# A fused DeltaNet and SwiGLU kernel: a planner's search with stored moves is replaced by one stored order of all operations

## The chip, the core and the metric

The kernel runs on one core of one Trainium2 chip. The metric is device time in microseconds, the median of several executions; before the change it is 663.25 us (three executions, 663.02 to 663.70). Lower is better. The engines are TensorE (PE; PEld is its weight load), VectorE (DVE), ScalarE (ACT), GpSimd (POOL) and SyncE (SP), which here only issues DMAs.

## What is computed

Two layers follow each other. The first is a DeltaNet recurrence over 4 batches x 8 heads, 768 steps, head size 48:

```
for t in range(S):
    y[:, :, t] = einsum('bhd,bhde->bhe', q[:, :, t], state)
    v_old = einsum('bhde,bhd->bhe', state, kt)          # kt: k[t], normalised
    state = state + bt * einsum('bhd,bhe->bhde', kt, vt - v_old)
```

Its output, turned to 3072 tokens x 384, goes through RMSNorm and a SwiGLU layer (384 to 1536 and back): `(silu(xn @ w_gate) * (xn @ w_val)) @ w_out`, in float32.

## The kernel before, in words

**Staging.** The sequence is cut into 12 chunks of 64 steps. For each chunk the recurrence is done in block form: scores of k with k and of q with k (PE, L705), the inverse of a unit triangular matrix (a chain of short DVE operations; for chunks 0 and 1 L904 and L914, later L1076 and L1085), products with the state and with that inverse, and the update of the state (PE, L1414). The chunk's output is normalised (ACT squares L1439, POOL roots L1464 and L1465), turned (PE L1495, evacuated by DVE L1499) and fed to the feed-forward layer: up products L1568 and down products L1550 for chunks 0 and 1, up products L1661 and down products L1718 (both by a scheme with fewer multiplications) for the other ten. The weights arrive from HBM as 64-bit words and are converted piece by piece by ACT (L620) and three DVE operations (L608, L611, L616 and a sum, L640).

**What sets the order.** The kernel does not issue instructions as it describes the work. It records 3005 operations by `P.add(engine, duration, function, priority, reads, writes, PSUM groups ...)`, and `Plan.run` then calls their functions in an order of its own. Operations are numbered as they are added, 0 to 3004, and the text below uses those numbers. Each engine executes its instructions in the order in which they were issued; semaphores between engines follow from the data. Before the change `Plan.run` searches: `forward` is a list scheduler with the model's durations, which gives PSUM banks to groups as they come free; `backward` and `reorder` make new priorities from its result; `shake` disturbs them from a stored number (`MOVES`, a long list of such numbers). The best of these orders by the model's end is issued.

**Fillers.** Up to 70 us by the model, `run` puts matmuls of the identity (L1836) into gaps of PE that the model expects: before each PE operation it compares the operation's modelled start with the end of the PE operation before (`pe = s + op.dur`), and fills the difference. They write a spare PSUM bank and read `ident`, which POOL makes at the start (`make_identity`, masks.py). The fillers are not operations of the plan.

**Row modes.** Matmuls use all 128 rows, or 64 or 32 (`P.rows`). The model charges a change of mode. Below, a stretch is a run of neighbouring PE operations in 64 or 32 rows between two in 128.

**The operations that the prediction speaks of.**

| number | engine, line in the profile | what it is |
|---|---|---|
| 4, 12, 13 | POOL masks.py, L540 and L543, L549 | `ident`; two masks |
| 18, 19 | ACT queue L488 | loads of the two halves of q of chunk 0 |
| 57, 59, 61 | PE L686, L686, L705 | turn k of chunk 0; its scores |
| 73, 75 to 97 | PE L849; DVE | gather, then the inversion of chunk 0 |
| 34 | DVE L608 | a shift in a weight's conversion |
| 120 to 137 | PE L1305, L1317; DVE L1365 (126 is one of these) | corrections of chunk 0, each waiting for the one before |
| 140, 157 | PE L1327, L1414 | output of chunk 0; state of chunk 0 |
| 141, 142, 149, 150 | ACT L1439 | squares of the output, two for each half |
| 145, 153; 146, 154 | POOL L1464, L1465; DVE L1470 | roots of the two halves; a diagonal made of each |
| 147, 155; 148, 156 | PE L1495; DVE L1499 | turned output of the two halves, and its evacuation |
| 452 | PE L1568 | first product of the feed-forward layer |
| 446, 449 | DVE L716, PE L705 | q of chunk 2 turned; its scores |

Of the kernel before, what the change touches and what calls it, by code (L numbers as in the profile page):

```python
# [25 lines left out]
ROUNDS, MOVES = (11, 17), (11000120, 11000520, 11000860, 11001126, 11001220, 11001422, 11001980, 11002920, 11003160, 11004760, 11005600, 11005880, 11005960, 11006540, 11006780, 11043348, 11046060, 11046762, 11046960, 11047400, 11051200, 11051587, 11052413, 11052800, 11052820, 11052943, 11053820, 11054160, 11059400, 11059520, 11065474, 11067742, 11067873, 11082899, 11089211, 11091393, 11091930, 11092484, 11092500, 11094487, 11095726, 11096934, 11097464, 11100744, 11101720, 11101800, 11103240, 11108560, 11111180, 11112100, 11113200, 11114320, 11115185, 11116472, 11119560, 11123118, 11123844, 11129946, 11130300, 11131636, 11133484, 11135300, 11135580, 11136720, 11137707, 11138500, 11141245, 11141565, 11141800, 11142243, 11143240, 11144659, 11145351, 11145392, 11145780, 11147877, 11159279, 11165300, 11166260, 11168180, 11184780, 11194240, 11199374, 11229385, 11245940, 11251680, 11259120, 11260740, 11758040, 11759220, 11773661, 11773860, 11778240, 11779680, 11781040, 11781305, 11781546, 11782138, 11783153, 11783560, 11792184, 11792893, 11794321, 11796160, 11800685, 11801080, 11823340, 11823372, 11824520, 11825640, 11826356, 11826483, 11826769, 11828197, 11829285, 11829840, 11829894, 11831880, 11837531, 11837960, 11840160, 11842020, 11858050, 11865880, 11866881, 11869703, 11870540, 11871293, 11871355, 11871362, 11871985, 11872236, 11872952, 11873062, 11873083, 11873496, 11874635, 11875943, 11876490, 11877075, 11877540, 11877667, 11879480, 11879491, 11879904, 11879920, 11880840, 11881540, 11881735, 11883480, 11884299, 11884640, 11885160, 11885407, 11885576, 11885889, 11886080, 11886591, 11886963, 11887410, 11887417, 11887780, 11890320, 11891127, 11891657, 11891671, 11891936, 11892084, 11892108, 11892132, 11892631, 11893543, 11895220, 11896940, 11899177, 11899762, 11900189, 11900750, 11937706, 11937985, 11938040, 11938200, 11939661, 11939723, 11939981, 11940060, 11940560, 11940660, 11941080, 11941260, 11941571, 11941681, 11941805, 11941840, 11942094, 11942342, 11942397, 11942428, 11942545, 11942989, 11944696, 11946950, 11953520, 11957695, 11957953, 11958514, 11958552, 11958996, 11959144, 11959433, 11959674, 11960951, 11961240, 11961505, 11961801, 11961911, 12010011, 12010360, 12010414, 12010548, 12011298, 12012255, 12012420, 12012480, 12014554, 12014688, 12015074, 12015201, 12015411, 12015948, 12017200, 12018092, 12018178, 12018202, 12026500, 12027260, 12028280, 12028861, 12031263, 12032385, 12233004, 12233496, 12235764, 12236425, 12237578, 12238320, 12239154, 12239254, 12240228, 12241157, 12241412, 12241522, 12241935, 12308180, 12308572, 12309120, 12309284, 12309540, 12310460, 12310578, 12310695, 12311566, 12311820, 12311831, 12311879, 12312571, 12313342, 12315200, 12315658, 12315665, 12316480, 12317785, 12319360, 12320084, 12320332, 12320440, 12321900, 12322710, 12322882, 12325601, 12325687, 12328265, 12328554, 12329420, 12331555, 12333379, 12336108, 12337380, 12338140, 12338789, 12339901, 12341329, 12341477, 12341501, 12349040, 12350398, 12351375, 12352232, 12354040, 12361697, 12365640, 12376020, 12377201, 12377349, 12379139, 12379314, 12379875, 12380261, 12380340, 12380581, 12380860, 12381180, 12382200, 12382322, 12383802, 12384153, 12384542, 12389320, 12393700, 12397307, 12397830, 12399723, 12400040, 12400370, 12400400, 12400480, 12401240, 12401867, 12402280, 12404120, 12446660, 12449007, 12449038, 12449960, 12449981, 12450820, 12451454, 12452820, 12453130, 12453822, 12453839, 12455133, 12455360, 12455701, 12455983, 12456427, 12457525, 12460237, 12460360, 12462320, 12463760, 12469433, 12472286, 12475683, 12476700, 12477872, 12478481, 12481785, 12485027, 12486160, 12487302, 12490040, 12496240, 12517588, 12518070, 12518335, 12519612, 12520680, 12520840, 12520860, 12520868, 12521866, 12521983, 12522427, 12522575, 12522699, 12522840, 12522878, 12523573, 12523728, 12523852, 12524060, 12524282, 12524296, 12524920, 12525022, 12525080, 12526160, 12526760, 12528973, 12530236, 12531080, 12532067, 12534380, 12546480, 12546818, 12548938, 12548955, 12551939, 12556444, 12557400, 12558140, 12562040, 12585099, 12858147, 12862253, 12862270, 12862525, 12862938, 12863096, 12863564, 12863943, 12865316, 12867209, 12868059, 12868854, 12869081, 12869790, 12870320, 12871308, 12871332, 12871463, 12871614, 12872010, 12872127, 12872430, 12873108, 12874698, 12877706, 12877768, 12878360, 12878377, 12878625, 12878828, 12878838, 12878976, 12879080, 12879788, 12879809, 12879984, 12880652, 12881674, 12882280, 12883646, 12885195, 12885732, 12886062, 12886730, 12888320, 12888480, 12888967, 12890457, 12890705, 12890746, 12890853, 12891018, 12891159, 12891717, 12892016, 12892749, 12894133, 12894518, 12896253, 12896435, 12897671, 12898490, 12898662, 12898669, 12899200, 12899636, 12899901, 12900166, 12900916, 12900947, 12901102, 12902434, 12902458, 12902885, 12903188, 12903439, 12903745, 12904048, 12904120, 12906901, 12906994, 12907049, 12908615, 12914686, 12915509, 12916073, 12921776, 12927995, 12955200, 12956175, 12956223, 12956760, 12957204, 12957899, 12957930, 12958123, 12958746, 12959441, 12959720, 12959761, 12960126, 12960694, 12961131, 12961678, 12962660, 12962800, 12962807, 12962900, 12962986, 12963251, 12963399, 12963554, 12964077, 12964841, 12967360, 12967646, 12970220, 12970520, 12972495, 12973166, 12975434, 12975613, 12979820, 12981144, 12981815, 12982080, 12984090, 12985088, 12986489, 12986661, 12987215, 12988344, 12989218, 12989648, 12993358, 12994012, 12994711, 12994852, 12995461, 12995974, 12996755, 12997134, 12997151, 12998280, 12998297, 13002372, 13002413, 13002802, 13003518, 13003893, 13005077, 13005373, 13005769, 13006200, 13006440, 13007211, 13007930, 13009080, 13010880, 13010907, 13011038, 13011616, 13011640, 13012284, 13012879, 13012996, 13013500, 13013557, 13015388, 13015980, 13017570, 13018262, 13019377)  # L26
BLOCK, ASKED, LACKED = 256, 140, 193
REACT, TURN, LAND = 2.4, 3.45, 2.6
STICK = 1.0
# [5 lines left out]
SHAKE = 0.12  # L35
# [37 lines left out]
class Plan:  # L73
# [39 lines left out]
    def first_priorities(self):  # L113
        for op in reversed(self.ops):
            if op.late:
                op.prio = min(
                    (u.prio - (0.0 if u.eng == op.eng and not op.dma else op.lat + u.slack + 0.2) for u in op.users),
                    default=op.prio,
                ) - STRETCH[op.eng] * op.dur - (3.0 if op.dma else 0.0)
            op.key = op.prio - op.ahead - (2000.0 if op.first else 0.0)  # L120

    def forward(self, banks, until):

        at = dict.fromkeys(ENGINES, 0.0)
        held = {"DVE": 0.0, "POOL": 0.0}
        cand = {e: [] for e in ENGINES}
        free = list(banks)
        for op in self.ops:
            op.wait, op.at = len(op.deps), op.ready
            for g in op.acquire:  # L130
                g.taken, g.uses = False, g.left
                g.reader, g.until = "", 0.0
            if not op.wait:
                cand[op.eng].append(op)
        order, server, end_, mode, slip = [], 0.0, 0.0, 0, 0.0
        self.lag = 0.0
        chain = {e: [] for e in ENGINES}
        for op in self.ops:
            op.was, op.done = op.start, False
            if op.first and op.was is not None:  # L140
                chain[op.eng].append(op)
# [1730 lines left out]
```

## Time and profile before

| | |
|---|---|
| median of three executions | 663.25 us |
| profiled execution, first to last instruction | 659.72 us |
| around it (663.25 less 659.72) | 3.53 us |
| PE busy | 649.0 us, 98% |
| weight loads busy | 603.6 us, 91% |
| DVE busy | 568.3 us, 86% |
| ACT, POOL busy | 295.5 us, 75.0 us |
| DMA issues on SP | 601 |

The profiled execution's own time is not listed apart from its span; its span and the median of the others differ by the 3.53 us that lie around a span. Busy times are sums over the span; a matmul's end is modelled, so the distance from the start of one PE operation to the start of the next says more about PE than its busy share, and the prediction uses such distances, read from the trace. "idle before" names the time that an engine stood still and what ended it.

### The profile page before, as it was taken

The numbers are of one execution on the slowest core, as the hardware profiler recorded it, in microseconds if no ns is written. First come the engines' busy times: TensorE is split into PE (matmuls) and PEld (weight loads), VectorE is DVE, ScalarE is ACT, GpSimd is POOL, SyncE is SP. The second block draws the span as 40 slices with busy tenths as digits, with TensorE's granted clock in tenths as the row PEclk, the third lists the DMA queues.
The fourth block names the chain that finished last, engine by engine and source line by source line (L and its number), as shares of the span: only waits on it lengthen the run. The fifth ranks groups of instructions, "written<-read, shape, count | busy, mean of one in ns | idle before, by whom it ended". The sixth has DMA issues, their size and how long they took to land.

```text
span 659.7 us, 23463 instructions
## 1 busy us (share of the span) xinstructions
PE 649.0 (98%) x10048; PEld 603.6 (91%) x10048; DVE 568.3 (86%) x1211; ACT 295.5 (45%) x681; POOL 75.0 (11%) x95
## 2 busy tenths in 40 slices
PE   8989999999999999999999999999999999999997
PEld 6878877777899999999999999999999999999997
DVE  5999999899899898998998998998999599367372
ACT  7555443224445545345355355345355353353241
POOL 4212201112011030110030120030021001000000
PEclk9999999999999999999999999999999999999999
DMA  9586593524526457466366385376345524301100
GB/s 229 132 214 162 124 246 115 95 35 94 93 42 109 68 135 110 65 153 110 52 152 107 57 164 93 68 154 98 59 110 80 97 46 74 58 26 25 25 1 25
DMA packets 270431, 64.40 MB, mean 98 GB/s; under 512 B 256980, under 2 KB 262135, under 8 KB 270327
## 3 DMA queue, kind: packets, MB, share of 16 engines
q1 hardware_dynamic: 267046, 62.12, 47.2%
q8 instruction: 79, 1.29, 0.8%
q10 hardware_dynamic: 3280, 0.79, 0.6%
q14 instruction: 26, 0.20, 0.1%
HBM read 45.30 MB, written 17.56 MB: 95 GB/s over the span
## 4 chain that ended last, share of the span: by engine, by line
PE 86%; DVE 9%; SPq 2%; issue 1%; ACT 1%; DMA 0%; POOL 0%; POOLq 0%; ACTq 0%; DVEq 0%
PE bank L1661 41%; PE bank L1718 21%; PE bank L1568 6%; PE bank L1550 4%; PE bank L1209 3%; PE bank L705 3%; SPq L488 2%; PE bank L1327 2%; PE bank L1291 2%; PE bank L1414 1%; PE bank L1836 1%; PE bank L1134 1%; PE bank L1162 1%; DVE tmp L616 1%; DVE w_in L640 1%
## 5 line engine op out<-in xcount | busy, mean ns | idle before, releaser
L1661 PE MATMUL bank<-xf,w_in 128*128 128x128 f32 x1440 | 177.4, 276 | 0.0
L1661 PEld LDWEIGHTS bank<-xf,w_in 128*128 128x128 f32 x1440 | 168.8, 192 | 0.9
L1671 DVE TENSOR_TENSOR tmp<-tmp,bank 128x512 f32<-128x512 f32 x180 | 121.3, 682 | 36.9 <-PE bank L1661 32.9
L1661 PE MATMUL bank<-xf,more 128*128 128x128 f32 x960 | 123.4, 277 | 0.0
L1661 PEld LDWEIGHTS bank<-xf,more 128*128 128x128 f32 x960 | 114.9, 192 | 1.3 <-issue 0.2
L1673 ACT COPY tmp<-bank 128x512 f32<-128x512 f32 x120 | 69.1, 585 | 72.2 <-PE bank L1661 52.4
L1677 ACT ACTIVATE tmp<-tmp 128x256 f32<-128x256 f32 x120 | 49.8, 417 | 92.1 <-DVE tmp L1671 91.8
L1085 DVE TENSOR_REDUCE acc<-acc 128x30 f32<-128x90 f32 (+4 forms) x150 | 69.8, 466 | 1.6
L732 POOL TENSOR_TENSOR knrm<-ksum,half 128x16 f32<-128x16 f32 x12 | 35.8, 2983 | 297.0 <-DVE ksum L731 297.0
L1718 PE MATMUL bank<-wo_sb,hf 128*128 128x192 f32 x360 | 63.7, 328 | 0.2 <-DVE hf L1678 0.2
L1718 PEld LDWEIGHTS bank<-wo_sb,hf 128*128 128x128 f32 x360 | 58.1, 190 | 0.8 <-DVE hf L1678 0.4
L1678 DVE TENSOR_TENSOR hf<-tmp 128x256 f32<-128x256 f32 x120 | 50.1, 428 | 9.1 <-ACT tmp L1677 8.4
L1076 DVE TENSOR_TENSOR acc<-acc,at 128x60 f32<-128x60 f32 (+4 forms) x150 | 51.3, 342 | 1.4
L1568 PE MATMUL bank<-xf,w_in 128*128 128x256 f32 x144 | 34.1, 384 | 0.3 <-DVE xf L1499 0.3
L1550 PE MATMUL bank<-wo_sb,hf 128*128 128x384 f32 x96 | 33.3, 488 | 0.0
L1568 PE MATMUL bank<-xp,w_in 128*128 128x256 f32 x144 | 32.9, 381 | 0.2 <-DVE r L1256 0.2
L1106 POOL COPY acc<-acc 128x128 f32<-128x128 f32 x40 | 21.0, 555 | 100.1 <-DVE acc L1085 86.9
L1568 PEld LDWEIGHTS bank<-xf,w_in 128*128 128x128 f32 x144 | 26.7, 190 | 5.3 <-issue 0.6
L1568 PEld LDWEIGHTS bank<-xp,w_in 128*128 128x128 f32 x144 | 27.0, 190 | 4.7 <-DVE r L1256 0.3
L1550 PEld LDWEIGHTS bank<-wo_sb,hf 128*128 128x128 f32 x96 | 17.9, 190 | 9.9
L1575 ACT ACTIVATE tmp<-bank 128x256 f32<-128x256 f32 x24 | 9.2, 383 | 38.8 <-PE bank L1568 36.7
L1520 DVE TENSOR_TENSOR xf<-xf 128x256 f32<-128x256 f32 (+1 forms) x70 | 24.0, 382 | 2.8 <-ACT xf L1505 1.2
(198 smaller groups left out, 967.0 us busy)
## 6 DMA issues: line engine op xcount, KB each, us to landing
at<-dkk SPq DMA_DIRECT2D x20, 256.0 KB, 3.7
more<-in_moe_w_gate_dram SPq DMA_DIRECT2D x6, 768.0 KB, 7.9
vt<-in_v_dram SPq DMA_DIRECT2D x24, 192.0 KB, 4.4
k<-in_k_dram SPq DMA_DIRECT2D x23, 192.0 KB, 3.9
out_dram<-tmp SPq DMA_DIRECT2D x46, 96.0 KB, 2.2
more<-in_moe_w_val_dram SPq DMA_DIRECT2D x5, 768.0 KB, 4.3
more<-in_moe_w_out_dram SPq DMA_DIRECT2D x5, 768.0 KB, 5.3
dsq<-k SPq DMA_DIRECT2D x6, 512.0 KB, 2.8
```

Of the source, the lines that this page charges most:

```text
L732: P.add("POOL", 2.95, lambda: nc.gpsimd.tensor_tensor(out=knrm[i2], in0=ksum[i2], in1=half, op=ALU.pow), pn, r=[("ksum", i2), "half"], w=[ ...
L1076: nc.vector.tensor_tensor(out=acc[:, 1:3, 0:n, j + 2 : W].rearrange("p a i t -> p i a t"), in0=acc[:, old, 0:n, j : j + 2, None].to_broadc ...
L1085: nc.vector.tensor_reduce(out=acc[:, new, 0:n, j + 2 : W], in_=acc[:, lo : lo + 3, 0:n, j + 2 : W].rearrange("p a i t -> p i t a"), axis=A ...
L1520: P.add("DVE", V(128 * n), lambda dst=dst, a=a, b_=b_, op=op: nc.vector.tensor_tensor(out=dst, in0=a, in1=b_, op=op), pxv, r=[("xp", 0)], ...
L1550: nc.tensor.matmul(po[p].t[:, 0:DM], hf[:, spot(f), 128 * p : 128 * p + 128], wo_sb[:, spot(f)], start=(f == f0), stop=(f == f1 - 1), skip ...
L1568: nc.tensor.matmul(ps.t[:, TOK * side : TOK * side + TOK], w_in[:, side, h_, 3 * t + i_, n : n + 128], x_[:, 2 * t : 2 * t + 2].rearrange( ...
L1661: nc.tensor.matmul(g.t[:, 128 * z : 128 * z + 128], fac[:, side, 128 * f : 128 * f + 128], xf[:, xs], start=(begin and z == 0), stop=False ...
L1671: P.add("DVE", V(512), lambda t=t, g=g: nc.vector.tensor_tensor(out=t, in0=t, in1=g.t, op=ALU.add), -1, r=[g], w=[tk], last=g)
L1673: P.add("ACT", A(512), lambda t=t, g=g: nc.scalar.copy(t, g.t), -1, r=[g], w=[tk], last=g)
L1677: P.add("ACT", A(256), lambda t=t: nc.scalar.activation(out=t[:, 0:256], in_=t[:, 0:256], func=ACTF.Silu), -1, w=[tk])
L1678: P.add("DVE", V(256), lambda t=t, f0=f0, p=p: nc.vector.tensor_tensor(out=hf[:, spot(f0) : spot(f0) + 2, 128 * p : 128 * p + 128], in0=t[ ...
L1718: nc.tensor.matmul(g.t[:, 0:192], a_[:, f], b_[:, f], start=(begin and f == 0), stop=(f == 5), skip_group_check=True)
```

## The change

No operation is added or taken away, and no duration, buffer or DMA is changed. `MOVES` and the search (`first_priorities`, `forward`, `backward`, `reorder`, `shake`) go. A string `ORDER` lists all 3005 operations, and `run` goes through it once, keeping the model's clock only to hand out PSUM banks and to place the fillers. Three details of `run` differ too: the time from which a filler is counted is now the modelled end with everything in it (`pe = end`, which includes a wait for PE's own instructions and a change of mode) and not `s + op.dur`; the bank that came free first is taken by the same model; and the bank release is timed by that end.

```diff
-ROUNDS, MOVES = (11, 17), (11000120, 11000520, 11000860,
...
+ORDER = """
+17 1 13 16 5 12 7 0 4 77 2 3 10 11 6 19 8 15 18 31 9 22 213 14 50 51 57 52 59 32 58 53 60 54 55 61 106 63 62 108 38 64 107 73 69 21 56 70 67 20 203 74
...
+"""
...
-    def run(self, free, filler=None, until=0.0):
-        self.first_priorities()
...
-        for op, s in best[1]:
-            op.start = s
...
-            if filler and op.eng == "PE":
-                if s < until:
-                    filler(fillers(pe, s))
-                pe = s + op.dur
-            op.fn()
...
+        for op in (self.ops[int(n)] for n in ORDER.split()):
+            e = op.eng
+            s = max(op.at, at[e])
...
+            end = s + op.dur
+            if e == "PE":
...
+                if s < until:
+                    n = fillers(pe, s)
+                    filler(n)
+                    count += 4 * len(n)
+                if op.size:
+                    late, asked = supply(s, op.dur, count, op.size)
+                    count += op.size + (0.5 if op.size in (16, 128) else 0.0)
+                    end += late
+                pe = end
...
+            op.fn()
```

What moves, by a comparison of the two programs as built: on PE 286 of 570 operations stand at another place, by 9 places at most; on DVE 970 of 1176, by up to 53; on ACT 345 of 615, by up to 8; on POOL 6 of 43, by up to 2; on SP 544 of 601, by up to 39. The largest DVE shifts lie between 60 and 190 us. The fillers are 14 matmuls instead of 16, with 3840 columns instead of 4608. Lines of the new kernel are 58 lower (the filler is L1778).

In the front of the program these moves matter to the text below:

```
            before                                  after
POOL        4, 12, 13                               13, 12, 4
ACT         77 213 (18 19: DMAs) 10 52              77 10 (19 18: DMAs) 213 52
DVE         84 34 85 ... 97                         84 85 ... 97
DVE         97 to 126, 34, 215 and 216 not in it    97 to 126, with 34, 215 and 216 in it
ACT         141 142 161 149 150                     141 142 149 150 161
DVE         148 164 156                             148 156 ... 164
PE          157, filler (768 columns), 147 155      157 147 155
PE          481 482 627 449 340 344 630             481 344 340 482 449 630 627
SP          last two q loads behind second at       all q loads of chunk 2 ahead of second at
```

More of the change, by code (lines that the diff above doesn't have):

```diff
@@ L2 @@
 import math
-import random
 from contextlib import ExitStack
@@ L111, in add, with run, supply @@
         return op
[L113 to L122, printed above, removed]
+    def run(self, banks, filler=None, until=0.0):
         at = dict.fromkeys(ENGINES, 0.0)
         held = {"DVE": 0.0, "POOL": 0.0}
-        cand = {e: [] for e in ENGINES}
-        free = list(banks)
+        free = sorted(banks, key=lambda x: x[0])
         for op in self.ops:
-            op.wait, op.at = len(op.deps), op.ready
+            op.at = op.ready
             for g in op.acquire:
[L131 to L141, printed above, removed]
-        for e in ENGINES:
-            chain[e].sort(key=lambda op: -op.was)
-        count, asked, usable = 0.0, -9.0, {}
-        def supply(s, dur, n0, size, keep):
+                g.uses = g.left
+        server, mode, count, asked, usable, lanes, pe = 0.0, 0, 0.0, -9.0, {}, [0.0] * 8, 0.0
+        def supply(s, dur, n0, size):
             late, last, got = 0.0, asked, {}
@@ L161, in supply @@
                         late += max(0.0, got.get(k, usable.get(k, 0.0)) - t)
[L162 to L163 removed]
+            usable.update(got)
             return late, last
[L165 to L200 removed]
@@ L201, in forward @@
+        for op in (self.ops[int(n)] for n in ORDER.split()):
+            e = op.eng
+            s = max(op.at, at[e])
+            if op.dma:
+                s = max(s, lanes[0])
+            for g in op.banks:
+                if g.reader != e:
+                    s = max(s, g.until)
+            if op.port:
+                s = max(s, held["POOL" if e == "DVE" else "DVE"])
             for g in op.acquire:
-                if not g.taken:
-                    g.taken = True
-                    free.pop(0)
@@ L205, in forward @@
-            op.start = s
+                if g.t is None:
+                    t, g.t = free.pop(0)
+                    s = max(s, t)
             if op.mode is not None and op.mode != mode:
                 s += DRAIN if op.mode < 128 else REFILL
-                op.start, mode = s, op.mode
+                mode = op.mode
             end = s + op.dur
-            if op.eng == "PE":
+            if e == "PE":
                 if s - at["PE"] > 1.4 and s > until:
@@ L345 @@
+                u.at = max(u.at, (end + TIED if e == "DVE" and not u.loose else at[e]) if u.eng == e and not op.dma else end + op.hop(u) + u.slack)
+        self.end = max(at.values())
 @with_exitstack
```

145 lines of the change are left out of this document (6 added, 139 removed), and 92 rows, old and new, of the table ORDER.

## The prediction

> **What bounds the kernel now.** First the stretches of the span, with each engine's busy time (columns: PE, PEld, DVE, ACT, POOL, granted clock, DMA share, GB/s).
>
> ```profile
> 6.90:20.00 13.10, 11.83 (x277) 9.25 (x275) 9.50 (x33) 10.44 (x19) 2.92 (x1) 1.00 0.91 226
> 20.00:41.00 21.00, 18.44 (x527) 16.35 (x528) 19.98 (x51) 10.55 (x26) 6.13 (x7) 1.00 0.73 189
> 41.00:100.00 59.00, 57.80 (x1085) 48.48 (x1085) 56.62 (x109) 29.06 (x59) 7.39 (x4) 1.00 0.71 181
> ...
> 150.00:655.00 505.00, 504.77 (x7779) 487.26 (x7778) 430.79 (x908) 224.53 (x536) 47.90 (x63) 1.00 0.45 83
> ```
>
> From 150 to 655 us PE is never idle (504.77 of 505 us): whatever order its instructions have, it does the same matmuls, and only a price that depends on its neighbours can change. Before 41 us PE waits for a chain, and from 20 us DVE is full (19.98 of 21). So an order can gain in the first 41 us, by changes of row mode, and by the few waits left. From the first up product (452, at 40.74 us) the starts add up to 613.0 us; the shortest distances seen for the same operation with the same neighbours add up to 606.0.
>
> Next the timeline of the start and of 33 to 41 us (start, duration, engine and line; in brackets the idle time before).
>
> ```profile
> 0.79 0.20 POOL masks.py:197 MEMSET ident<- 128x128 f32 x1 [0.29 <-POOLq L1856]
> ...
> 1.07 0.29 POOL masks.py:199 TENSOR_SCALAR_AFFINE_SELECT ident<-ident 128x128 f32<-128x128 f32 x1
> ...
> 1.31 0.10 POOL L540 MEMSET below<- 128x3 f32 x1
> ...
> 1.42 4.21 PE L1836 MATMUL bank<-ident 128*128 128x512 f32 x6 [1.42 <-POOL below L540]
> 1.49 0.42 POOL L543 TENSOR_SCALAR_AFFINE_SELECT below<-below 64x3 f32<-64x3 f32 x2
> ...
> 1.96 0.31 POOL L549 MEMSET wsum<- 128x256 f32 x1
> ```
>
> PE starts as soon as `ident` is done, and its first six filler records hold it until 5.42, when 57 starts; k had landed at 5.08.
>
> ```profile
> 33.83 0.26 PE L1414 MATMUL bank<-u,k 64*48 64x48 f32 x4
> 35.58 0.92 PE L1414 MATMUL bank<-u,k 64*48 64x48 f32 x60 [1.49 <-issue]
> 36.43 1.57 PE L1836 MATMUL bank<-ident 128*128 128x512 f32 x6
> 37.84 0.39 PE L1495 MATMUL bank<-xp,yn 128*128 128x128 f32 x2
> ```
>
> Operation 157 stops after four matmul records for its own instructions, takes 2.60 us to the next start where a later one takes 0.83, and then a filler keeps 147 back for 1.41 us, although its inputs were there at 35.66.
>
> ```profile
> 35.39 0.33 ACT L1439 ACTIVATE xp<-bank 128x192 f32<-128x192 f32 x1 [0.51 <-DVE acc L914]
> ...
> 39.18 0.95 DVE L616 SCALAR_TENSOR_TENSOR more<-hf,more 128x768 f32<-128x768 uint32 x1
> ...
> 40.05 0.55 DVE L1499 TENSOR_TENSOR xf<-bank,g_sb 128x384 f32<-128x384 f32 x1
> ...
> 40.74 1.97 PE L1568 MATMUL bank<-xf,w_in 128*128 128x256 f32 x8 [0.27 <-DVE xf L1499]
> ```
>
> The last evacuation (156) stands behind a weight conversion: its matmuls ended at 39.39, it starts at 40.05.
>
> **The change part by part.** Durations are those of the profiled execution.
>
> *1. `ident` made third (+0.85).* On POOL L549 (0.31), L540 (0.10) and L543 (0.42) now stand ahead; with the gaps between (0.1 us in all) `ident` is ready 0.93 later, so the first filler starts at 2.35. It is the same filler (4.0 us), so 57 starts near 6.3 instead of 5.42. 57, 59, 61, the spread of the scores (L775, L777), the gather and the inversion hang on it one behind another. Cover: q of chunk 0 lands at 9.33, and 108 holds back the gather now; that hides 0.2 at the gather, but ACT's four operations behind 61 shift fully. Between 0.4 and 0.93; I take 0.85, near full, as the chain has no other slack.
>
> *2. DVE between 14 and 31 us (+0.5).* Taking shift 34 (0.55) out of the inversion frees 0.38 (85 started at 15.48 and could at 15.10). But 97 (end 19.98) to 126 (29.82) is DVE without a pause, and there 34, 215 and 216 come in: 0.55 + 0.39 + 0.25, less 0.09 of overlap each, = 0.92. So 126, and with it 127 to 157, comes 0.92 - 0.38 = 0.5 later. Between 0.4 and 0.6.
>
> *3. No filler after 157 (-1.4) and the second half's evacuation (-0.5).* With 1 and 2, 157 starts at 33.83 + 1.35 = 35.2, and with the same stop ends at 37.8; 147 follows at once: 37.8 against 37.84. The second half: ACT does 149 and 150 straight behind 140 (35.4 to 36.2, no waiting for DVE), POOL's root 153 follows 145 (36.65 + 1.57 = 38.2), 154 takes 0.28, 155 starts at 38.6 (38.51 before) and ends 0.88 later. 156 follows at 39.5, not behind the 0.95 of L616, and 452 starts at 40.2 instead of 40.74. The first three parts together: **-0.5**. The stop in 157 has the same instructions ahead of it (11 filler matmuls before and after the change), so I keep 1.77; without it the chain over 154 binds and at most 0.4 more would come.
>
> *4. Fewer changes of row mode (-1.2).* A group of L1661 starts 0.893 after its like, but needs 0.987 ahead of a 64-row operation and 0.995 behind one; scores (L705) take 1.091 ahead of 128 rows and 0.982 ahead of another 64-row operation. So a stretch joined to another saves 0.094 + 0.102 + 0.11 = 0.31. From 452 on there are 62 stretches before and 58 after: 4 x 0.31 = 1.2. If the 32-row ones save only the first two, 0.8.
>
> *5. The scores of chunk 2 (-0.4).*
>
> ```profile
> 80.17 0.58 SPq L488
> ...
> 80.80 0.45 SPq L488
> ...
> 81.29 3.15 DMA vt<-in_v_dram
> 84.44 0.02 issue
> 84.45 1.24 DVE qt L716
> ```
>
> Their turned q (L716) waits for the last two q loads, which SP issues behind the second load of `at` (78.80, 1.32 us); 627 ahead of 449 takes 2.24 instead of 0.97, a wait of 1.27. With all q loads ahead of that load the wait is gone; but 344 and 340 move ahead of 482, and 344 needs ACT's result of 83.30, when PE, 0.5 early, is there at 81.6 with the old times. ACT shifts early with the rest by 0.5, so some 0.9 to 1.2 comes back. Between -1.27 and +0.4; I take -0.4.
>
> *6. The rest (0).* DVE and SP are mixed most between 60 and 190 us. PE's waits there, besides that of part 5, are 0.25, 0.23 and 0.1 us, though DVE stands idle for only 2.4 us between 41 and 100. The two loads of k that hold SP from 84.7 to 93.7 are issued some 35 us later, which clears the queue. The cover gone would cost up to those 2.4 us. The tail (3.9 us behind the last PE operation) only swaps two stores between queues: 0.
>
> Sum: -0.5 (parts 1 to 3, at 452) - 1.2 - 0.4 = **-2.1 us**. The span of 659.72 becomes 657.6; with 3.53 us around it, and against the median of 663.25, **661.2 us**. A difference of 0.2% (1.33 us) is about what this measurement can tell from none.
>
> **The clock.** The first filler's 512-column records start 0.85 apart, later ones 0.43, and the L686 records change from 0.213 to about 0.11 at 6.7 us: PE runs at half speed for 5.3 us after its first matmul (1.42). [...]
>
> **Rivals.** *A, q later (to 663.6).* ACT now issues the q loads behind a second table load and an activation; if the queue holds them until those are done (copy to 3.47, table 1.28, activation 0.20), they go at 5.0 and 5.6 instead of 1.64 and 2.30. Landing is then between 10.2 (the first load's 4.64 us) and 12.6 (the second's 7.03); the gather follows 1.1 behind, at 13.7 instead of 11.3 at worst: 0 to +2.4. Against: at 1.64 the queue has already passed a table load and two copies. [...] Chance 0.1.
>
> *B, full clock later (662.7).* If the later first matmul delays full speed past the gather, 61 and 106 to 73 run at half speed: about +1.1 for 61 and +0.4 for what of the others isn't hidden, so -0.6. Against: nothing in one trace shows the rise moving by more than the start does. [...] Chance 0.07.
>
> *C, nothing to gain (662.6).* PE is full from 41 us and parts 3 and 5 turn into other waits: only part 4 is left, less 0.5: -0.7. For it: 41 to 100 us, DVE 96% busy. Chance 0.12.
>
> *D, slower (664.7).* PE stops for its own instructions where dense 64-row operations follow one another, as in 157: 1.77 us each time. The new order has four runs of three (before: one of three, one of four); two such stops make -2.1 + 3.5 = +1.4, and from two on it is slower. Against: other runs of 64 rows (two L705 at 350 us, 2.02 us together) pass without a stop. Chance 0.12.
>
> *E, the late start costs little (659.9).* If q's landing or the clock's rise hides half of it, part 1 falls to 0.4 (-0.45); with part 5 in full (-0.87 more) that is 659.9. Chance 0.14.
>
> **How the numbers follow.** Forecast 661.2, chance 0.45 with 660.3 to 661.9. Faster by over 0.2% (under 661.92): 0.45 + E 0.14 = 0.59. Within 0.2%: A, B, C = 0.29. Slower (over 664.58): D 0.12. Range 659.4 (E, and no stop in 157) to 664.0, which leaves out most of D and little else.
>
> **What will show it.** First filler (L1778) at 2.35 and L628 at 6.3; no L1778 between L1356 and L1437 near 37.8; first L1510 near 40.2; ACT's L1381 four in a row; the last PE operation about 2.1 us earlier. Wrong if the gather (L791) comes after 12 us (A), if L1603 groups show idle "issue" above 1 us (D), or if PE stands waiting for DVE by more than 1 us in all between 41 and 165 us (C).

## The result, and the profile after

| | before | after |
|---|---|---|
| median, 22 executions each | 663.26 us | 666.09 us |
| lowest, highest | 661.75, 667.19 | 662.98, 669.44 |
| profiled execution, span | 659.72 us | 663.3 us |
| start of operation 452 | 40.74 us | 39.73 us |
| start of the last PE operation | 653.74 us | 657.33 us |

The ratio is 1.0035 (95% interval 1.0021 to 1.0050): slower by 0.35%, where 661.2 us was forecast and the range ended at 664.0. In the profiled executions the new order gains 1.0 us up to operation 452 and loses 4.6 us behind it.

In the new kernel scores are L647 (they were L705), the turns (transpositions) of loaded q and k on DVE L658 (L716), the up products L1603 (L1661), the DVE sums that feed them L1613 (L1671). First the stretches, with the columns of the prediction's first fence.

```profile
20.00:41.00 21.00, 18.35 (x530) 16.68 (x530) 19.66 (x50) 10.94 (x28) 6.34 (x7) 1.00 0.64 181
41.00:100.00 59.00, 57.13 (x1141) 47.57 (x1140) 54.86 (x106) 29.77 (x60) 7.59 (x4) 1.00 0.62 156
150.00:655.00 505.00, 500.79 (x7745) 483.12 (x7736) 429.11 (x904) 223.05 (x534) 47.29 (x63) 1.00 0.46 82
```

In the stretch where PE was never idle before (504.77 of 505 us) it now stands 4.21 us. The start, and 33 to 41 us, in the timeline:

```profile
1.69 0.20 POOL masks.py:197 MEMSET ident<- 128x128 f32 x1
1.96 0.29 POOL masks.py:199 TENSOR_SCALAR_AFFINE_SELECT ident<-ident 128x128 f32<-128x128 f32 x1
...
2.31 3.69 PE L1778 MATMUL bank<-ident 128*128 128x512 f32 x6 [2.31 <-POOL ident masks.py:199]
...
34.40 0.26 PE L1356 MATMUL bank<-u,k 64*48 64x48 f32 x4
...
35.05 0.92 PE L1356 MATMUL bank<-u,k 64*48 64x48 f32 x60 [0.39 <-issue]
...
36.28 0.94 PE L1437 MATMUL bank<-xp,yn 128*128 128x128 f32 x6 [0.31 <-DVE xp L1412]
...
39.73 1.53 PE L1510 MATMUL bank<-xf,w_in 128*128 128x256 f32 x6
```

`ident` comes late, as the diff said; no filler stands between 157 (L1356) and 147 (L1437) any more, and 452 (L1510) starts a microsecond earlier. What PE waited for behind 41 us, by the view of waits (engine, line, releaser: us in total, times, longest):

```profile
PE bank L1104 <- DMA mt<-dx: 1.3, 1, 1.3
PE bank L647 <- DVE qt L658: 1.2, 1, 1.2
PE bank L647 <- DVE kt L658: 1.0, 1, 1.0
PE bank L1603 <- DVE tmp L1613: 0.9, 1, 0.9
PE bank L1104 <- ACT tmp L1665: 0.5, 1, 0.5
PE bank L1076 <- DMA m1bd<-dxt: 0.4, 1, 0.4
...
```

The same view of before has four lines:

```profile
PE bank L705 <- DVE qt L716: 1.1, 1, 1.1
PE bank L1568 <- DVE xf L1499: 0.3, 1, 0.3
PE bank L1718 <- DVE hf L1678: 0.2, 1, 0.2
PE bank L1568 <- DVE r L1256: 0.2, 1, 0.2
```

In the changed kernel the second is operation 449 at 85.6 us, which had its wait in the trace of before as well. The other five of those shown lie between 261 and 467 us, where the kernel before has none above 0.2. The table gives each operation's step, the distance from the start of the PE operation ahead of it to its own start:

| operation | starts at | step: shortest of all traces with this PE order, and here | what ended the wait |
|---|---|---|---|
| 1253, L1076 | 261.6 us | 2.05, 2.54 us | loads of `m1bd` |
| 1314, L1603 | 298.0 us | 0.89, 1.97 us | DVE, which stood at a turn |
| 1912, L647 (scores) | 351.7 us | 0.99, 2.07 us | DVE's turn 1911, behind loads from `dsq` |
| 1866, L1104 | 366.6 us | 2.04, 2.57 us | ACT |
| 2366, L1104 | 467.2 us | 2.15, 3.56 us | a DMA |

Together the five steps are 4.6 us above the shortest. (The other steps behind 452 gain and lose some 0.8 us each, so that the loss there is 4.6 us too.)

Operation 1314 in the timeline:

```profile
288.01 2.46 SPq L430 DMA_DIRECT2D q<-dsq  x3
...
290.58 1.57 SPq L430 DMA_DIRECT2D dyn<-yn  x2
...
292.19 0.56 SPq L430 DMA_DIRECT2D q<-dsq  x1
...
293.71 0.68 DVE L1613 TENSOR_TENSOR tmp<-tmp,bank 128x512 f32<-128x512 f32 x1
...
296.09 1.25 DVE L658 STREAM_TRANSPOSE kt<-q 128x1024 f32<-128x1024 f32 x1 [1.70 <-DMA q<-dsq]
297.25 3.04 DVE L1613 TENSOR_TENSOR tmp<-tmp,bank 128x512 f32<-128x512 f32 x5
...
297.96 1.16 PE L1603 MATMUL bank<-xf,more 128*128 128x128 f32 x8 [0.91 <-DVE tmp L1613]
```

SP issues the last of four q loads behind two stores of yn. DVE stands 1.70 us at the turn (operation 1661) until that load has landed, and the L1613 group behind it starts only then, at 297.25 us. PE needs neither load nor turn there: it needs the L1613 that stands behind the turn. The kernel before has the same DVE operations around the turn, and no wait:

```profile
294.99 1.24 DVE L716 STREAM_TRANSPOSE kt<-q 128x1024 f32<-128x1024 f32 x1
296.15 2.61 DVE L1671 TENSOR_TENSOR tmp<-tmp,bank 128x512 f32<-128x512 f32 x4
```

New are the times: the last q load was issued at 290.97 us before, at 292.19 in the changed kernel, and DVE came to the turn at 294.99 us before, at 294.39 in the changed kernel.

### The profile page after: what moved, and what is told of

Read it like the earlier page. It is cut to its first block, busy times and chain, and to the rows that moved or that the text cites. A ratio compares the mean times of both kernels' runs of the same rounds, so it can differ in the third digit from the quotient of the medians.

```text
span 663.3 us, 23462 instructions
## 1 busy us (share of the span) xinstructions
PE 646.5 (97%) x10044; PEld 601.3 (91%) x10044; DVE 569.9 (86%) x1211; ACT 294.8 (44%) x681; POOL 74.8 (11%) x95
## 4 chain that ended last, share of the span: by engine, by line
PE 84%; SPq 5%; DMA 4%; DVE 3%; issue 2%; ACT 1%; POOL 1%; ACTq 0%; DVEq 0%
PE bank L1603 36%; PE bank L1660 20%; PE bank L1510 8%; SPq L430 5%; PE bank L1492 4%; PE bank L647 3%; PE bank L1151 3%; PE bank L1269 2%; PE bank L1233 2%; DMA q<-dsq 1%; PE bank L1356 1%; DMA vt<-in_v_dram 1%; PE bank L1104 1%; PE bank L1259 1%; PE bank L1076 1%
## 5 line engine op out<-in xcount | busy, mean ns | idle before, releaser
L1603 PE MATMUL bank<-xf,w_in 128*128 128x128 f32 x1440 | 178.6, 276 | 0.0
L1603 PEld LDWEIGHTS bank<-xf,w_in 128*128 128x128 f32 x1440 | 169.4, 192 | 0.9 <-issue 0.2
L1613 DVE TENSOR_TENSOR tmp<-tmp,bank 128x512 f32<-128x512 f32 x180 | 121.7, 681 | 37.8 <-PE bank L1603 30.8
L1603 PE MATMUL bank<-xf,more 128*128 128x128 f32 x960 | 124.8, 277 | 0.9 <-DVE tmp L1613 0.9
L1603 PEld LDWEIGHTS bank<-xf,more 128*128 128x128 f32 x960 | 115.2, 192 | 2.6 <-DVE tmp L1613 1.1
L1510 PE MATMUL bank<-xf,w_in 128*128 128x256 f32 x144 | 33.8, 384 | 0.1
L1510 PE MATMUL bank<-xp,w_in 128*128 128x256 f32 x144 | 33.0, 382 | 0.3 <-DVE hf L1518 0.3
L1510 PEld LDWEIGHTS bank<-xf,w_in 128*128 128x128 f32 x144 | 26.6, 190 | 5.6 <-issue 0.5
L1510 PEld LDWEIGHTS bank<-xp,w_in 128*128 128x128 f32 x144 | 26.9, 190 | 5.0 <-DVE hf L1518 0.7
```

The source lines that it names most:

```text
L1510: nc.tensor.matmul(ps.t[:, TOK * side : TOK * side + TOK], w_in[:, side, h_, 3 * t + i_, n : n + 128], x_[:, 2 * t : 2 * t + 2].rearrange( ...
L1603: nc.tensor.matmul(g.t[:, 128 * z : 128 * z + 128], fac[:, side, 128 * f : 128 * f + 128], xf[:, xs], start=(begin and z == 0), stop=False ...
L1613: P.add("DVE", V(512), lambda t=t, g=g: nc.vector.tensor_tensor(out=t, in0=t, in1=g.t, op=ALU.add), -1, r=[g], w=[tk], last=g)
```

## Experiments

All kernels use the changed `run`, so an experiment is another `ORDER` (noq and pool also change the issue of some DMAs). "Old" and "new" are the two orders; a part of one is followed by what is left of the other, in its own sequence. Ratios are against the kernel before, on the same chip.

**Theory:** the five waits between 245 and 480 us are the loss, and they come from the order there. **Rivals:** the start (late `ident`, fewer fillers, the clock); the details of `run`; the order of PE alone or of SP alone.

### Where the loss lies

```diff
 border     ORDER = old
 fa_rb      ORDER = new up to 452         + rest of old
 fb_ra      ORDER = old up to 452         + rest of new
 a250_b     ORDER = new up to 245 us      + rest of old
 bab        ORDER = old up to 452, new up to 245 us, rest of old
 bba        ORDER = old up to 248 us      + rest of new
```

> The order of the kernel before, written out as ORDER in the changed kernel's run. Theory (the waits of the new order between 41 and 655 us): nothing of the loss is left, the median within 1 us of before's 663.3, last PE start near 653.7 us. Rival (the details of run: counting of fillers with pe = end, banks handed out by the same clock): 665 us or more, and the fillers of the start differ.

> The new order up to operation 452 (the first up product), then what is left in the order of before. Theory: only the gain at 452 stays (39.73 against 40.75 us, so -1.0), less about 0.3 where the two orders are joined: 662.3 to 663 us. Rival (the later ident, the missing filler and the clock at the start cost the time): 665 to 666 us, and executions at a granted clock of .995 as often as in the changed kernel (7 of 22).

> The order of before up to operation 452, then what is left in the new order. Theory: the whole loss of the middle without the gain of the front: 2.8 + 1.0 over before, 667 us, with waits for DMA at the same operations (1314, 1912, 2366). Rival (the start): 663.3 us. If the waits hang on the 1 us by which 452 comes earlier, PE here would be late enough for the DMAs and most of the waits would shrink: 664 to 665 us.

> The new order up to the 245th us of its model, then what is left in the order of before. Theory: the loss arises behind 250 us (waits of 0.4, 1.1, 1.2, 0.5 and 1.5 us between 259 and 464 us), so those go and the balance at 250 us (about 0, with the front's -1.0 and +1.0 behind it) stays: 662.5 to 663.7 us. Rival (the start, or the waits at 54 and 77 us, carry it): 665 us or more.

> Old order up to operation 452, new order up to 245 us, old order behind. If the gain of the kernel with the new order up to 245 us (660.4) is made in the first 41 us alone, this one is like before, 662.7 us or a little slower (the trace of the old front with the new order behind it lost 1.0 us between 41 and 250 us: 663.7). If the new order between 41 and 245 us gains by itself: 661.5 us or below.

> Old order up to 248 us, new order behind. Theory (the new order behind 245 us loses by itself): before plus 2 to 3 us, 665 to 666 us. Rival (it loses only where the new order stands ahead of it, by 1 to 2 us of earlier work): 663 us.

> The new order up to 245 us and the old behind it, timed a second time. First time 660.4 us, ratio to before 0.9966 (0.9948 to 0.9985). If that was no chance: 660 to 661 us, and in the trace again no wait over 0.5 us behind 100 us.

| to 41 us | 41 to 245 us | behind | run | median | ratio (95%) |
|---|---|---|---|---|---|
| old | old | old | border | 662.62 us | 0.9986 (0.9970 to 1.0003) |
| new | old | old | fa_rb | 663.13 us | 1.0001 (0.9983 to 1.0019) |
| old | new | old | bab | 662.90 us | 0.9996 (0.9979 to 1.0014) |
| new | new | old | a250_b | 660.36 us | 0.9966 (0.9948 to 0.9985) |
| new | new | old | a250_b2 | 661.08 us | 0.9978 (0.9951 to 1.0005) |
| old | new | new | fb_ra | 664.43 us | 1.0018 (0.9995 to 1.0042) |
| old | old | new | bba | 665.51 us | 1.0032 (1.0010 to 1.0053) |
| new | new | new | after2 | 664.49 us | 1.0021 (1.0000 to 1.0042) |

The details of `run` show no cost (border). The new order behind 245 us costs 0.3% behind the old order (bba), 0.2% behind the front of bab (fb_ra against bab, whose intervals overlap) and 0.4 to 0.7% behind the new order (the changed kernel and after2 against a250_b2 and a250_b). The waits differ with what stands ahead: the step to 1314 is 1.3 us and that to 1912 0.9 us above the shortest in bba, which has no wait at 1253, and fb_ra waits 1.6 us at 1253 and 0.2 to 0.3 us at 1314, 1912 and 1866. The new order ahead of 245 us gains 0.3% in one timing and 0.2%, with an interval that reaches 1.0005, in the other; its first 41 us alone (fa_rb) and its middle alone (bab) show no gain. I had expected fa_rb to keep the 1.0 us, and fb_ra to take 667 us. In the trace of fa_rb 452 starts at 41.51 us (a clock dip, below); behind it PE has about 1 us of fillers at 47 to 49 us that the kernel before does not have there, 0.8 us of "issue" at 81 us (border has 1.4 at the same operation) and a wait of 0.7 us for DVE at 92 us. The waits of a250_b behind 41 us, all that the view lists:

```profile
PE bank L1356 <- issue: 0.4, 1, 0.4
PE bank L1510 <- DVE hf L1518: 0.4, 1, 0.4
PE bank L647 <- DVE qt L658: 0.2, 1, 0.2
PE bank L1660 <- DVE hf L1620: 0.2, 1, 0.2
```

None of the five is left, nor in a250_b2, where 449 waits 2.0 us at 86 us. So the start is not the cause; the loss is behind 245 us.

### The start: `ident` first again

```diff
-17 1 13 16 5 12 7 0 4 77 ...      (a250_b)
+17 1 4 13 16 5 12 7 0 77 ...      (a250_id)
```

> The kernel of the new order up to 245 us and the old behind it (660.4 us), with ident first on POOL again. The first filler starts at 1.4 instead of 2.3. By the price of the prediction's part 1: 0.85 less, 659.5 us. If the clock's rise and the landing of q hide most of it (57 started at 5.81 against 5.42): 0.4 less or nothing.

Measured: 661.91 us, ratio 0.9978 (0.9954 to 1.0002), no better than a250_b. 57 starts at 5.42 us, but 452 at 39.66, between the 39.39 and 39.91 of the traces of a250_b and a250_b2. No cost of the late `ident` is seen at 452 or in the time. That is one trace, though, and ten traces with the late `ident` and no clock dip spread from 39.39 to 40.51.

### One DVE instruction, two places later

```diff
-... 1289 1456 1285 1661 1307 1297 1313 ...    (DVE)
+... 1289 1456 1285 1307 1297 1661 1313 ...
```

> The changed kernel with one DVE instruction (1661, the square turn behind the q loads) moved behind the next two DVE operations, 1307 and 1297; SP's order unchanged. Theory (PE at 1314 waited because DVE stood in its order before 1661 for a DMA): PE's wait at 1314 falls from 1.07 to under 0.2 us, though the DMA lands no sooner; about 1 us earlier at operation 1320. Rival (the wait is PE's need of the turned k itself): it stays or moves to operation 1662.

> The changed kernel with the one DVE instruction (1661) two places later, now timed: in its one execution the waits at 1314, 1866 and 2366 were gone, and the span 660.9 against 663.3. If one place on DVE carries the later waits too: 663 to 664 us. If that was the chance of one execution (its 452 started 0.8 us later): -1.1 against the changed kernel, 665 us.

> The changed kernel once more, for its trace and its time beside the others. The waits at 1253, 1314 and 1912 (0.40, 1.07, 1.17 us) hang on the order and come again; those at 1866 and 2366 (0.51, 1.50 us), gone in two executions of a kernel with one DVE instruction moved, hang on long DMA issues that fall elsewhere each time, and are gone here. Time: 665 to 666.5 us. If they come again, the one DVE instruction at 296 us carries them.

Measured: turn296, one execution, 662.58 us; turn296b 663.75 us, ratio 1.0000 (0.9978 to 1.0023), against 1.0035 (from 1.0021) and 1.0021 (from 1.0000) for the changed kernel: the intervals overlap, so the gain rests on the traces. From the timeline of turn296b:

```profile
293.49 0.56 SPq L430 DMA_DIRECT2D q<-dsq  x1
...
293.98 2.29 DVE L1613 TENSOR_TENSOR tmp<-tmp,bank 128x512 f32<-128x512 f32 x3
...
296.27 1.95 PE L1603 MATMUL bank<-xf,more 128*128 128x128 f32 x16
...
296.87 1.25 DVE L658 STREAM_TRANSPOSE kt<-q 128x1024 f32<-128x1024 f32 x1 [0.60 <-DMA q<-dsq]
```

The load is issued 1.3 us later than in the changed kernel, and PE no longer waits: DVE does the L1613 first that PE needs. So PE waited because DVE stood at the turn, as the theory had it. The DVE order is not what is new there, as the kernel before has the turn at the same place: what is new is a later load and an earlier DVE, and an earlier load cures the wait as well (fix4 and spB, below). In both traces of this kernel the step to 1314 is 0.89 us, and the 0.5 us at 1866 are gone too. Whether those hung on the same stall is open: the steps to 1314 and 1866 are 2.19 and 2.08 us in bba, 1.18 and 2.49 us in noq. In after2, the changed kernel again, the steps to 1314 (2.38 us), 1912 (2.07), 1866 (2.44) and 1253 (2.44) come again; the 1.4 us at 2366 do not (2.15 us, as in ten of the 13 traces with that PE order; two show 2.24 and 2.41). The longest wait of the profiled execution was chance.

### The order of SP

```diff
 spB     PE, ACT, DVE, POOL: new; SP behind 245 us: old
-new     ... 1416 1221 1415 1143 1417 1418 1225 1226 ...
+fix4    ... 1225 1226 1416 1221 1415 1143 1417 1418 ...
-new     ... 1387 1386 1659 ...
+fix4    ... 1659 1387 1386 ...
-new     ... 1735 1910 1639 1908 1909 1907 ...
+fix4    ... 1910 1908 1909 1907 1735 1639 ...
-new     ... 2141 2224 2419 2223 2213 2221 2222 ...
+fix4    ... 2224 2223 2221 2222 2141 2419 2213 ...
 spEt    SP behind 245 us sorted by the start of each DMA's first user; 1661 behind 1307 1297 (DVE)
```

> The changed kernel, with the DMAs behind the 245th us of the model issued on SP in the order of before, and PE, ACT, DVE and POOL as in the changed kernel. Theory (SP's order makes the loss behind 250 us): the waits of 0.4, 1.2 and 1.5 us for DMAs at operations 1253, 1912 and 2366 and the 1.07 us at 1314 go, about -4, near 662 us or below. Rival (the order of the computing engines): they stay, 665 to 666 us. Where both orders must fit each other, new waits come at other places and the time lies between or above.

> The changed kernel with ten DMAs moved by a few places on SP, at four places: the m1bd loads of 1253, the last q load of 1661, the q loads of 1911, the x2bd loads of 2366. Theory: the four waits shrink from 0.40, 1.07, 1.17 and 1.50 us to under 0.3 each: -3.0 to -4.1, 662 to 663 us. If the waits move to what now stands behind (dkk, yn), the trace shows new ones of like size and the time stays at 665 us.

> The changed kernel, behind 245 us of the model, with SP's order put anew by the time at which the first user of each DMA started in the trace of the changed kernel (325 DMAs move, by 19 places at most), and the turn 1661 two places later on DVE; PE, ACT, POOL as in the changed kernel. Theory (SP's order costs the waits): the four waits go and no new one over 0.5 us comes, 661 to 662 us. Rival (no order of SP serves this order of PE; what is moved forward is paid for by what is moved back): 664 to 666 us, with new waits for DMAs.

Measured: spB 666.89 us, ratio 1.0060 (1.0034 to 1.0086); fix4 664.75 us, 1.0030 (1.0012 to 1.0048); spEt 679.18 us, 1.0226 (1.0183 to 1.0268). In spB and fix4 the DMA waits at 1253 and 1912 and the stall at 1314 are gone; in their place stands one larger wait, in spB 3.3 us at 521 us, in fix4 this one:

```profile
362.54 1.08 PE L1076 MATMUL bank<-m1bd,kk 128*32 128x64 f32 x32 [2.44 <-DMA m1bd<-dxt]
```

It is operation 1753. PE stood there 1.2 us earlier than in the changed kernel (358.0 against 359.2 us at the PE operation ahead), and its two loads were issued 1.1 us later (359.7 and 360.2 against 358.6 and 359.1 us): fix4 had put two DMAs behind the q loads, one of them 1639 (from 343.0 to 347.3 us), a load of yn that 1640 and 1641 follow one behind another, and all behind it on SP came later. What was moved forward was paid for by what was moved back. So SP's order alone is not the cause: with the new order of the other engines the old order of SP is no better, the moves of fix4 give nothing that the intervals show, and sorting by the first user's time is 13 us worse (its trace also has half clock in four stretches of 3.41 us, below, by an estimate from half speed at most 6.8 us of it).

### Fewer DMAs on SP

```diff
 noq     the 16 loads of q of each chunk from 4 on: not issued
 pool    the 16 loads of q and 2 of v of each chunk from 4 on: nc.gpsimd, not nc.sync
```

> The changed kernel without the loads of q from chunk 4 on (16 DMAs of each chunk on SP, 128 of 601 in all; q then holds old data, everything else as before in the same order). Theory (SP's queue is the limit that the new order runs into, its issues of 0.5 to 2 us stand in front of the DMAs that the recurrence waits for): the waits at 1253, 1314, 1912 and 2366 shrink together by 2.5 us or more, 663 us or below. Rival (the order of the computing engines alone): the waits stay, 665 to 666 us.

> The changed kernel with the loads of q and v from chunk 4 on issued by POOL and not by SP (144 of SP's 601 issues), all data as before. Theory (issue on SP): the same waits shrink as without the loads, 663 to 664 us, if POOL's own work (11% busy) is not held up. Rival (the transfers themselves, not their issue): the waits shrink without the loads, but not here.

Measured: noq 661.75 us, ratio 0.9965 (0.9945 to 0.9986); pool 673.38 us, 1.0134 (1.0097 to 1.0171). Without the loads the steps to 1314 and 1912 shrink to 1.18 and 1.09 us (1.97 and 2.07 in the changed kernel), those to 1253 (2.77) and 1866 (2.49) do not; the load on SP and the DMA engines thus feeds two of the waits. Pool can't say which of the two it is: POOL's busy time goes from 74.8 to 161.9 us, its q loads stand in the chain that ended last (2%), and PE waits 4.6 us for L1613 and 3.1 us for turns. That run is inconclusive. Noq's gain is also larger than the traces explain: the steps named shrink by 1.6 us in all against the changed kernel. Part of it may be the clock: its mean was 0.998 or more in 11 of the 12 executions of noq, in 22 of 34 of the changed kernel.

### Repairs that move back only what can wait

```diff
 fix2    1661 behind 1307 1297 (DVE)
 fix2    1225 1226 ahead of 1416 (SP)
 fix2    loads of v 1734 1735 behind 1723 (SP; from 341 and 347 us to 361 us, first user at 369 us)
 fix3    fix2, and on PE 1755 1912 where the new order has 1912 1755
```

> The changed kernel with three repairs: the turn 1661 two places later on DVE; the m1bd loads of 1253 ahead of four dkk stores; the two loads of v that stand among the q loads of 1911 moved behind them, by 16 us, since their first user starts 25 us later. Theory (what is moved back must have time to spare): the waits at 1253, 1314 and 1912 go and nothing new comes at 1753, where the earlier repair paid 2.4 us back: -2.6 against the changed kernel, 663 to 663.5 us. Rival (SP has no order that serves this PE order): a new wait of 1 to 2 us, 664.5 to 666 us.

> The three repairs, and a fourth: on PE the scores 1755, whose inputs are there, one place ahead of 1912, which waits 1.0 to 1.2 us for the turn 1911 in every execution of this order. Theory (PE takes up 1912 too soon behind the turn's DMA): 1755 fills the wait, -1.0 against the three repairs, 662 us. If 1755 itself must wait or what comes behind shifts the wait: 663 us as with three.

Measured: fix2 662.99 us, ratio 0.9994 (0.9974 to 1.0015); fix3 662.14 us, 0.9989 (0.9969 to 1.0009). The steps to 1253, 1314 and 1866 are 2.05, 0.89 and 2.04 us in both; the wait at 1912 stays in fix2 (1.89 us: the issue of the last q load, 1907, takes 2.2 us by itself) and goes in fix3 (0.98), where 1755 fills it. Before had 1755 ahead of 1912 too. The view of waits of fix3:

```profile
PE bank L1603 <- DVE tmp L1613: 0.7, 1, 0.7
PE bank L1104 <- issue: 0.2, 1, 0.2
PE bank L647 <- DVE qt L658: 0.2, 1, 0.2
```

The first is new, at 383 us. The intervals are too wide to part neighbours: the fourth repair's own gain is seen in the trace, not in the times. The four repairs together are apart from the first timing of the changed kernel (0.9989 with an upper end of 1.0009 against 1.0035 with a lower end of 1.0021), but not from after2 (from 1.0000).

## Why the prediction was wrong

**Step 6, "The rest (0)", failed.** It looked for waits in the trace of before, found three small ones between 60 and 190 us, and rested on the prediction's first reading, "From 150 to 655 us PE is never idle", as if that were a property of the stretch. It was a property of the old order there. The new one issues the last q load of a turn so late that DVE stops at it (1661), puts scores on PE directly behind a turn (1912, ahead of which before had 1755), and puts one of the two loads that 1253 needs nine places later on SP. The step bounded a lost cover by 2.4 us, DVE's idle time between 41 and 100 us, and looked nowhere behind 190 us. In its place the runs show waits between 245 and 480 us of 4.6 us in one trace of the changed kernel and 3.4 us in the other. The trace of before had a warning that I did not read: from the issue of the last DMA that an operation needs to the start of that operation, the median between 245 and 480 us is 10.7 us, and 8 of the 81 such operations on PE, DVE and ACT have under 4 us. (Nothing tells from this alone which will stall: in the changed kernel it is 6.8 us and 16, but fix3 still has 6.4 us and 15.)

**Parts 1 to 3: the sum right, a term wrong.** The first filler came at 2.31 us (2.35 forecast), and 57 at 6.30 or 6.31 us in 12 of 14 traces with the new front (6.3), at 5.8 in two. In the ten of these traces whose clock did not dip ahead of 452, 452 started at 40.07 us on average, against 40.60 in the four of the old front (the fifth, fb_ra, has a dip): -0.53 for -0.5. But part 1's 0.85 is not seen at 452 (a250_id), and neither is the -1.4 of the filler: border has the old order without a filler behind 157, and there 147 starts at 36.16 us (37.84 before) but 452 at 40.56 (40.74), since 155 waits until 38.48 for the second half's diagonal. So the terms of parts 1 to 3 are not confirmed one by one, and that they add up is in part luck. The stop in 157 came again, shorter (0.39 us of "issue" for 1.49). That PE lacked its own instructions there, and the stops of rival D with it, was my reading: the traces show only that PE waited for nothing the profile lists.

**Part 4** fits at its lower bound: the PE steps behind 452 that changed by at most 0.15 us each sum to between -0.7 and -1.0 us in the two traces of the changed kernel, depending on how a step is counted (-1.2 forecast, -0.8 as its bound). What else is small is in that sum too, and bab, with the same 58 stretches, shows no gain in time.

**Part 5**'s gain did not come. The scores of chunk 2 wait 0.3 to 2.1 us in the 16 traces with the new order there, 1.1 on average, and 0 to 1.5 us, 0.75 on average, in the four with the old. All q loads are indeed ahead of the second load of `at`, but the last of them is issued no sooner (at 80.92 us, before at 80.80), its issue takes 0.4 to 1.6 us on SP in these traces, and the turn waits for it:

```profile
78.30 3.94 SPq L430 DMA_DIRECT2D q<-in_q_dram  x6
82.28 0.48 SPq L430 DMA_DIRECT2D at<-dkk  x1
...
84.27 1.25 DVE L658 STREAM_TRANSPOSE qt<-q 128x1024 f32<-128x1024 f32 x1 [2.76 <-DMA q<-in_q_dram]
```

**The sum without step 6.** The kernel that has the new order only up to 245 us is what parts 1 to 5 spoke of (it has the 58 stretches too): 2.3 and 1.3 us below the kernel before beside it, 2.1 forecast. With part 5 missing, that is not a confirmation of each part.

**Rivals.** C ("nothing to gain", PE's waits turn into others) came nearest in kind, but named 41 to 100 us and +1.4 on the forecast. A is false: the q loads were issued at 1.68 us, and the gather started at 9.88 against 10.46. D's sign did not come: no L1603 shows idle "issue" above 1 us. Idle "issue" did come elsewhere, 1.47 us at 15 us in the changed kernel (0.44 in after2) and 1.4 us at 79 us in border, but none of the five waits is one. B (full clock later) and E (the late start costs little) depend on the execution, not on the order: the first record of full clock lies between 5.27 and 8.29 us in the 14 traces with the new front (6.92 in that of before), and of the ten without a dip 452 starts at 39.4 to 39.9 us in the four where it came before 6.6 us, at 39.9 to 40.5 in the six where it came after 7.9. The 3.53 us around the span was a wrong reading: in 21 of the 22 executions of the changed kernel time less span is 1.7 to 2.1 us, so the profiled execution of before was probably one of the shorter ones; the forecast went by the change against the median, which that does not touch.

## What to carry over

When a whole order is exchanged, that PE was full before (504.77 of 505 us) does not show that it is full in the new order (500.79): compare, per stretch, on each engine what now stands directly behind a DMA's landing (turns on DVE, scores on PE) and what is queued behind it. The stall of DVE at 1661 no longer held PE when the turn stood two places later (step to 1314 0.89 us for 1.97, turn296b), nor when its load came earlier on SP (PE's wait for `tmp` of L1613 at most 0.2 us in fix4 and 0.3 in spB, 0.9 in the changed kernel). What moves back on SP needs time to spare: in fix4 operation 1753, which PE reached 1.2 us earlier than in the changed kernel, waited 2.44 us for two loads issued 1.1 us later, while the two loads of v that fix2 moved back to 361 us have their first user at 369 us, and its view of waits lists none for a DMA. And exchange the orders by stretches: it found a combination 0.2 to 0.3% faster than before (clear of noise in one of two timings) in a change that was 0.3% slower.

## What was unexpected of the hardware

**PE's clock fell behind a single long wait in fix4, spB and pool.** The stretches of fix4 around its 2.44 us wait:

```profile
350.00:358.00 8.00, 8.00 (x182) 7.81 (x181) 7.67 (x15) 5.38 (x13) 0.00 (x0) 1.00 0.70 107
358.00:363.00 5.00, 2.56 (x34) 2.29 (x36) 4.33 (x12) 2.24 (x6) 0.00 (x0) 0.92 0.70 105
363.00:368.00 5.00, 5.00 (x45) 4.83 (x38) 1.91 (x7) 0.38 (x1) 0.00 (x0) 0.74 0.60 142
368.00:376.00 8.00, 8.00 (x217) 7.30 (x218) 7.32 (x16) 2.94 (x8) 0.00 (x0) 1.00 0.17 22
```

The granted clock is 0.74 in the 5 us behind the wait, and the next two operations take 1.4 us longer than without it; so this wait of 2.4 us cost 3.8. The same in spB (3.3 us, then 0.66) and pool (2.9 us, then 0.71). Waits of 2.0 and 2.1 us (a250_b2 at 86 us, pool at 353 us) show 1.00 in the stretch behind them. Cut at the edges of the clock's records, fix4 has 1.00 from 358.82 to 362.23 us, with PE busy for 1.28 us of them, then 0.50 up to 365.64 us, then 1.00 again. Every dip ahead of the end lasts 3.41 us in these traces (twice 6.82), and begins a whole number of such stretches behind the first record of full clock in its trace. PE was busy for 0.12 us (spB), 0.55 us (pool) and 1.28 us (fix4) of the stretch ahead of these dips; the wait in a250_b2 lies across an edge at 85.02 us, PE is busy for 1.92 us of the stretch behind that edge, and no dip follows. So the stretch ahead of a dip was not idle throughout in any of the three. Waits of 2.4, 2.9 and 3.3 us had a dip behind them in these runs, waits of 2.0 and 2.1 us had none; whether the length of the wait decides, or how much of it falls into one stretch, is open.

**Dips without such a wait.** In fa_rb, fix2, fix3 and fix4 the clock is 0.82 to 0.84 between 12 and 20 us (0.50 for 3.41 us from 17.1 to 17.5 us on), with the same order there as in ten traces that show no dip; 452 then starts at 41.4 to 41.7 us, 1.5 later on average. PE was busy for 2.1 to 2.3 us of the stretch ahead of these dips; in the changed kernel it was busy for 2.07 us of one (15.58 to 18.99 us), and no dip followed. So what starts such a dip is open. Every kernel timed more than once has executions with a mean granted clock of 0.997 or less (12 of 34 of the changed kernel, 19 of 34 of the kernel before in one batch), which is much of the spread in the times: in the first 22 executions of the changed kernel their median is 668.3 us, that of the others 665.0.

**DMA issue on SP** took 0.5 us in the middle between 245 and 480 us (0.49 in the trace of before, 0.50 in that of the changed kernel) but over 1.2 us for 12 to 21 of the 200 to 285 issues there (18 of 283 and 20 of 275 in these two), at other operations in each execution. What makes them long is open too.
